# Three more chunks' low parts loaded ahead of a branch, and a prefetch hint for the branch, in an attention and two-expert-layer kernel

## The chip, the cores and the metric

The kernel runs on one core of one Trainium2 chip, in one launch. The metric is the time of an execution on the device in microseconds (us). Three runs of the kernel before gave 924.8, 921.22 and 925.86 us; their median, 924.8 us, is the time before. The engines are PE (TensorE: matmuls, with its weight loads listed as PEld), DVE (VectorE), ACT (ScalarE), POOL (GpSimd) and SP (SyncE, which issues nearly all DMAs). Each runs its own list of instructions in order and waits on semaphores for the others.

## The reference

The input goes through three layers. What is computed, cut to its core:

```python
# 1 linear attention: 4 batches, 8 heads, 576 positions, 64 wide, 128 random features
phi = lambda x: exp(x @ omega.T - (x*x).sum(-1)/2 - rowmax) / sqrt(128)
x = (phi(q) @ (phi(k).T @ v)) / (phi(q) @ phi(k).sum(0) + 1e-6)      # 2304 tokens x 512
# 2 a dense layer, hidden width 2048
h = x @ w_in
x = (h - tanh(h)) @ w_out
# 3 eight experts with room for 288 tokens each
logits = x @ w_gate
# all (token, expert) pairs by falling logit: a token goes to the first expert
# that still has room; then out[mask] = relu(x[mask] @ w1[e]) @ w2[e]
```

## The kernel before

**Precision.** Matmuls take operands as pairs: a high part, rounded to the matmul's format, and a low part, the rest. A product is three matmuls: high by high, high by low, low by high. So a name often stands twice: `gH` and `gL` are the high and low parts of a hidden chunk, `wo` and `oL` those of a chunk of `w_out`, `wi` and `iL` those of `w_in`. The low parts of the weights lie in HBM as `low_wi` and `low_wo`; a chunk's 256 KB are loaded into a ring of three buffers (`iL`, `oL`) when the chunk is due.

**The dense layer.** The 2304 tokens are six blocks of 384 (`NBLK`), a block three tiles of 128 (`TPB`); the hidden width is 16 chunks of 128 (`NF`). Per chunk `chunk_ops` makes the hidden values from 12 matmuls (L601 to L603) and a polynomial in place of `h - tanh(h)`, `hidden_ops` splits them (L298 the high part, L303 the low part, on POOL or DVE), and `m2_ops` multiplies them by the chunk of `w_out`: nine matmuls of 512 columns (L648), three into each of three accumulators `acc`.

**The last two blocks.** Blocks 4 and 5 make their hidden chunks together, before a branch; what they yield is kept. Block 5's lie in buffers of their own (`gH5`, `gL5`). Block 4's high parts overwrite the chunk of `wi` that was just used, and its low parts go to HBM (L799, `g4l<-gL`), out of a ring of four buffers `gL`, and are read back (L821, `gL<-g4l`) when the second product of block 4 needs them. This second product is `but_last_ops`: chunks 0 to 2 (`NHERE = 3`) are multiplied ahead of the branch, chunks 3 to 15 behind it, and then block 5's 16 chunks in `last_ops`: 261 matmuls of L648 behind the branch. The gate logits of both blocks don't wait for it: `last_logits` (L719, L721) takes them from the hidden parts, chunk by chunk, and after the last chunk copies, transposes (L732) and adds them into `lg` (L736, L737).

**The branch.** The polynomial holds only for small values. `range_ops` works out a flag `over` in time, and at L1455 every engine loads it into a register (TENSOR_LOAD) and at L1456 compares and branches: with `over` above 0 into a block that computes the dense layer again in a general way, otherwise past it. With these inputs the general block is jumped over. In the program's memory it stands between the code ahead of the branch and the code behind it, and has some 1,860 matmuls and other instructions of PE.

**Behind the branch.** The routing (`best_ops`, `search_ops`, `route_ops`) settles the experts one after the other, p = 0 to 7. Each search has seven steps: DVE makes thresholds and compares (`r_cmp`, L1029), PE counts (L1035, nine matmuls `rp`), DVE turns the counts into a digit (`r_cond`), PE spreads it (L1060), DVE makes the next thresholds. PE runs matmuls of L648 between these steps. After search 0 the expert's weights are loaded (`load_ops`), the tokens get their places, the rows of `ms` are gathered by POOL (L1288, `r_xg`), transposed on PE (L1304) and go through the expert's two layers (`expert_ops`, first matmul L1332).

**What sets the order.** All of it is recorded as operations with a due time (`plan.at` plus a lag) and estimated durations. `Plan.run` then issues them one by one: the operation that can start earliest, and among equals the one due first. It picks the engine where there is a choice (POOL or DVE for a low part) and the buffer of a ring; an operation without a free buffer is not ready. So a change of a ring or of a due time moves instructions far from the place that was edited. The branch ends a run of the plan: nothing moves across it.

Of the kernel before, what the change touches and what calls it, by code (L numbers as in the profile page):

```python
# [8 lines left out]
F32 = mybir.dt.float32  # L9
F32R = mybir.dt.float32r  # L10
# [175 lines left out]
def tile_kernel(ctx, tc, q, k, v, omega, w_in, w_out, w_gate, w_gate_t, w1, w2, out, dbg=None):  # L186
    nc = tc.nc
# [4 lines left out]
    P = 128  # L192
    NT, DM = v.shape
# [72 lines left out]
    def sring(where, shape, dtype, name, n):  # L266
        return plan.ring(shape, dtype, name, [(where, [f"{name}{i}" for i in range(n)], False)])
# [14 lines left out]
                    sring(wat, [P, DM], F32R, "lw", 2))  # L282
    sqr = sring(wat, [P, DM], BF16, "sq", 1)
    iLr = sring(wmid, [P, DM], F32R, "iL", 3)
    oLr = sring(wout, [P, DM], F32R, "oL", 3)
    xHr = sring(wmid, [P, NC, BLK], F32R, "xH", 2)
    xLr = sring(wmid, [P, NC, BLK], F32R, "xL", 2)
    ur = sring(wmid, [P, BLK], F32, "u", 1)
    sr = sring(wmid, [P, BLK], F32, "s", 5)
    gHr = sring(wmid, [P, BLK], F32R, "gH", 2)  # L290
    gLr = sring(wkeep, [P, BLK], F32R, "gL", 4)
    xmr = sring(wout, [P, DM], F32, "xm", 3)
    g5r = [plan.ring([P, BLK], F32R, n, []) for n in ("gH5", "gL5")]
    mTr = sring(wmid, [P, NC, P], F32, "mT", 1)
# [422 lines left out]
    def last_logits(j, acc, f, prev, gH, gL):  # L717
# [20 lines left out]
                    w=[lgb], lag=8.9)  # L738
        return o

    LAG2, LEADX, LEADI, LEADO = 10.4, 15, 5.43, 4.91

    def mlp_ops(start, step, general=False):

        x, lacc, lprev = {}, Buf(kvr), None
        for b in acc4:
            b.slot[4] = None
        for j in range(NBLK - 1):
            for i in range(j, j + 1 if j < NBLK - 2 else NBLK):
                x[i] = Buf(xHr), Buf(xLr)  # L750
                for t in range(TPB):
                    plan.at = start[j] + (3.0 if i > j else -LEADX) + 1.5 * t
                    if i == j > 0 and not general:
                        plan.at = max(x_due[i * TPB + t] + 9.0, start[j - 1] + LEADX)
                    x_ops(i, t, *x[i], general)
            if j == NBLK - 2:
                break
            acc = [Buf(accr) for _ in range(TPB)]
            prev = None
            e0, e1 = ROWS.get(j, (0, 0))  # L760
            along = not general and e0 < e1
            if along:
                plan.at = start[j]
                rows, scratch = vg_rows(e0, e1 - e0, weight_rings[0]), Buf(weight_rings[2])
            for f in range(NF):
                plan.at = start[j] + step[j] * f - LEADI
                wsp = split_ops("wi", f)
                g = Buf(gHr), Buf(gLr)
                plan.at = start[j] + step[j] * f
                chunk_ops(j, f, x[j], wsp, general, *g)  # L770
                plan.at = start[j] + step[j] * f + LAG2 - LEADO
                wsp = split_ops("wo", f)
                if along:
                    vg_ops(f, e0, e1 - e0, rows, wsp[1], weight_rings[1], scratch)
                plan.at = start[j] + step[j] * f + LAG2
                prev = m2_ops(f, g, wsp, acc, prev)
            if along and e1 == E:
                vg_split()
            for t in range(TPB):
                plan.at = start[j] + step[j] * NF + LAG2 + 0.7 * t  # L780
                xm, _ = out_ops(j, t, acc[t])
                gate_ops(j, t, xm)

        j, lacc4, lprev4 = NBLK - 2, Buf(bank), None
        for f in range(NF):
            plan.at = start[j] + step[j] * f - LEADI
            wsp = split_ops("wi", f)
            if not general:
                g5.append((Buf(g5r[0]), Buf(g5r[1])))
            plan.at = start[j] + step[j] * f  # L790
            s4 = chunk_ops(j, f, x[j], wsp, general)
            plan.at += step[j] / 2
            chunk_ops(j + 1, f, x[j + 1], wsp, general, *g5[f])
            plan.at = start[j] + step[j] * f
            gH, gL = Buf(None, wi[:, f, :BLK]), Buf(gLr)
            gH.readers = list(wbuf["wi", f].readers)
            hidden_ops(s4, gH, gL)
            lprev4 = last_logits(j, lacc4, f, lprev4, gH, gL)
            g4[f] = gH, plan.op(SP, 0.47, lambda e, f=f, gL=gL: nc.sync.dma_start(g4l[f], gL.t.bitcast(F32)), r=[gL],  # L799
                                nbytes=P * BLK * 4, lag=6.8)  # L800
            plan.at += step[j] / 2
            lprev = last_logits(j + 1, lacc, f, lprev, *g5[f])

        new = [Buf(accr) for _ in range(TPB)]
        for b in new:
            b.left += 1
        for b, old in zip(new, acc4):
            b.want = old.slot
        acc4[:] = new
        but_last_ops(0, NHERE, start[j] + step[j] * NF + 1.0, 2.0)  # L810

    g4, acc4, prev4 = {}, [], [None]
    NHERE = 3

    def but_last_ops(f0, f1, start, step):

        for f in range(f0, f1):
            plan.at = start + step * f
            gH, st = g4[f]
            gL = Buf(gLr)  # L820
            plan.op(SP, 0.47, lambda e, f=f, gL=gL: nc.sync.dma_start(gL.t.bitcast(F32), g4l[f]), w=[gL], after=[st],  # L821
                    nbytes=P * BLK * 4)
            prev4[0] = m2_ops(f, (gH, gL), split_ops("wo", f), acc4, prev4[0] if f else [flags[-1]] * TPB)

    stored, stored4, m5 = [], [], []

# [623 lines left out]
    range_ops()  # L1450
    plan.at = T_MLP + 100.0
    plan.op("-", 0.0, lambda e: r_setup(), after=flags[:1])
    plan.run()
    s_pre.close()
    nover = nc.values_load(over[0:1, 0:1], min_val=0, max_val=1)  # L1455
    with tc.If(nover > 0), ExitStack() as s_gen:  # L1456
        wgen = pool(s_gen, "wgen", "left")
        gen[:] = [sring(wgen, [P, H, D], F32, "gx", 2), sring(wgen, [P, BLK], F32, "gd", 3)]
        gsum, gmask = sring(wgen, [P, DM], F32, "gw", 1), sring(wgen, [P, DM], F32, "gm", 1)
        grings = sring(wgen, [P, DM, 2], U32, "gr", 1), gsum, sring(wgen, [P, DM], F32R, "gl", 1)  # L1460
        zeros = wgen.tile([P, DM], F32, name="zeros")
        plan.op(DVE, 0.3, lambda e: nc.vector.memset(zeros, 0.0))
        plan.at = -300.0
        for f in range(NF):
            for kind in ("wi", "wo"):
                plan.at += 4.0
                weight_ops(kind, f, grings, (gmask, zeros))
        plan.run()
        bvg[0] = Buf(None)
        for e0 in range(0, E, 2):  # L1470
            plan.at += 10.0
            rows, scratch = vg_rows(e0, 2, grings[0]), Buf(grings[2])
            for f in range(NF):
                plan.at += 2.0
                vg_ops(f, e0, 2, rows, split_ops("wo", f)[1], gsum, scratch)
            plan.run()
        vg_split()
        mlp_ops([70.0 * j for j in range(NBLK)], [4.3] * NBLK, True)
        plan.run()
# [9 lines left out]
    plan.at = -100.0  # L1489
    AT_LAST, AT_W = -42.7, 1.09  # L1490
    but_last_ops(NHERE, NF, AT_LAST - 1.5 * NF, 1.5)
    for b in acc4:
        b.left -= 1
    but_ops = list(plan.ops)
    plan.at = AT_LAST
# [97 lines left out]
```

## Time and profile before

| what | us |
|---|---|
| median of three runs | 924.8 |
| the profiled execution | 925.26 |
| its span, first to last instruction | 923.5 |
| PE busy in the span | 881.9 (95%) |
| PE's weight loads busy | 774.0 (84%) |
| DVE busy | 655.3 (71%) |
| ACT busy | 467.5 (51%) |
| POOL busy | 251.4 (27%) |

Times in the rows further down are from the span's start, so the branch is at about 546. A timeline row gives start, duration, engine, line, operation, what is written and read, and in brackets how long the engine sat idle before it and what ended that. PE's matmuls are pipelined: a row's duration includes the fill, and what one costs in a row of equals is the distance between starts. The granted clock (PEclk) is the share of full speed that TensorE was given: 1.00 is 2.4 GHz, 0.50 is 1.2 GHz.

### The profile page before, as it was taken

The numbers are of one execution on the slowest core, as the hardware profiler recorded it, in microseconds if no ns is written. First come the engines' busy times: TensorE is split into PE (matmuls) and PEld (weight loads), VectorE is DVE, ScalarE is ACT, GpSimd is POOL, SyncE is SP. The second block draws the span as 40 slices with busy tenths as digits, with TensorE's granted clock in tenths as the row PEclk, the third lists the DMA queues.
The fourth block names the chain that finished last, engine by engine and source line by source line (L and its number), as shares of the span: only waits on it lengthen the run. The fifth ranks groups of instructions, "written<-read, shape, count | busy, mean of one in ns | idle before, by whom it ended". The sixth has DMA issues, their size and how long they took to land. (4 is left out here: it accounts for less than half of the span.)

```text
span 923.5 us, 17550 instructions
## 1 busy us (share of the span) xinstructions
PE 881.9 (95%) x6168; PEld 774.0 (84%) x6168; DVE 655.3 (71%) x1931; ACT 467.5 (51%) x1015; POOL 251.4 (27%) x271
## 2 busy tenths in 40 slices
PE   8988999999999999999999949899999999999995
PEld 6887888988988888989989926676888888999995
DVE  6998999866588789777878754516787786784520
ACT  5875564645457445654577630203366454465521
POOL 1122424333431346234313230010222322221211
PEclk9997999999999999999999978999999999999998
DMA  8987877776375766434677645744798887877600
GB/s 255 345 278 237 273 242 266 264 242 206 111 239 150 217 206 218 147 104 136 233 270 269 242 152 162 270 138 156 231 272 227 271 209 214 268 180 273 211 27 26
DMA packets 104371, 194.79 MB, mean 211 GB/s; under 512 B 28369, under 2 KB 42833, under 8 KB 104274
## 3 DMA queue, kind: packets, MB, share of 16 engines
q1 hardware_dynamic: 98610, 174.71, 57.8%
q0 software_dynamic: 5664, 18.88, 8.5%
q8 instruction: 50, 0.82, 0.4%
q14 instruction: 47, 0.39, 0.1%
HBM read 150.03 MB, written 34.08 MB: 199 GB/s over the span
## 5 line engine op out<-in xcount | busy, mean ns | idle before, releaser
L601 PE MATMUL bk<-xH,wi 128*128 128x384 f32 x320 | 114.9, 359 | 1.2 <-ACT phi L438 1.0
L648 PE MATMUL acc<-wo,gL 128*128 128x512 f32 x288 | 115.5, 403 | 0.0
L602 PE MATMUL bk<-xL,wi 128*128 128x384 f32 x320 | 109.0, 341 | 0.5 <-DVE xL L303 0.5
L603 PE MATMUL bk<-xH,iL 128*128 128x384 f32 x320 | 108.9, 340 | 0.0
L707 DVE SCALAR_TENSOR_TENSOR lw<-wf,raw 128x512 f32<-128x512 f32 x128 | 103.6, 809 | 2.1 <-POOL wf L704 0.7
L648 PE MATMUL acc<-wo,gH 128*128 128x512 f32 x240 | 100.5, 419 | 0.0
L303 POOL TENSOR_TENSOR gL<-s,gH 128x384 fp32r<-128x384 f32 x52 | 63.0, 1212 | 135.9 <-ACT gH L298 128.4
L438 ACT ACTIVATE phi<-bk,nm 128x128 f32<-128x128 f32 x272 | 76.9, 379 | 38.8 <-DVE nm L441 38.5
L648 PE MATMUL acc<-oL,gH 128*128 128x512 f32 x240 | 95.5, 398 | 0.3 <-DVE oL L303 0.3
L704 POOL TENSOR_TENSOR wf<-oL,wo 128x512 f32<-128x512 f32 x48 | 64.9, 1352 | 68.0 <-DMA oL<-low_wo 61.9
L626 DVE SCALAR_TENSOR_TENSOR s<-s,bk 128x384 f32<-128x384 f32 x80 | 44.0, 551 | 45.7 <-ACT s L625 45.0
L298 ACT ACTIVATE gH<-s 128x384 fp32r<-128x384 f32 x80 | 42.2, 527 | 60.4 <-DVE s L628 43.8
L601 PEld LDWEIGHTS bk<-xH,wi 128*128 128x128 f32 x320 | 61.2, 191 | 7.3 <-ACT phi L438 2.0
L648 PEld LDWEIGHTS acc<-wo,gL 128*128 128x128 f32 x288 | 55.0, 191 | 13.2 <-POOL gL L303 0.3
L602 PEld LDWEIGHTS bk<-xL,wi 128*128 128x128 f32 x320 | 61.4, 192 | 3.3 <-DVE xL L303 0.7
L605 ACT ACTIVATE u<-bk 128x384 f32<-128x384 f32 x80 | 39.1, 489 | 46.2 <-PE bk L603 45.3
L603 PEld LDWEIGHTS bk<-xH,iL 128*128 128x128 f32 x320 | 61.2, 191 | 0.0
L628 DVE SCALAR_TENSOR_TENSOR s<-s,u 128x384 f32<-128x384 f32 x80 | 56.3, 704 | 1.1
L441 DVE TENSOR_REDUCE nm<-bk 128x4 f32<-128x512 f32 (+1 forms) x75 | 46.4, 632 | 12.9 <-PE bk L427 12.1
L648 PEld LDWEIGHTS acc<-wo,gH 128*128 128x128 f32 x240 | 45.4, 189 | 6.9
L625 ACT ACTIVATE s<-u,qbias 128x384 f32<-128x384 f32 x80 | 49.3, 616 | 3.8 <-DVE gL L303 1.5
L648 PEld LDWEIGHTS acc<-oL,gH 128*128 128x128 f32 x240 | 45.5, 190 | 6.4 <-DVE oL L303 0.6
(355 smaller groups left out, 2354.9 us busy)
## 6 DMA issues: line engine op xcount, KB each, us to landing
r_wraw<-in_moe_w_dram SPq DMA_DIRECT2D x48, 512.0 KB, 5.5
iL<-low_wi SPq DMA_DIRECT2D x80, 256.0 KB, 2.7
oL<-low_wo SPq DMA_DIRECT2D x80, 256.0 KB, 2.8
raw<-in_moe_w_in_dram SPq DMA_DIRECT2D x32, 512.0 KB, 5.6
raw<-in_moe_w_out_dram SPq DMA_DIRECT2D x32, 512.0 KB, 4.8
dw<-in_moe_w_dram SPq DMA_DIRECT2D x16, 512.0 KB, 5.0
w1l<-dw SPq DMA_DIRECT2D x16, 512.0 KB, 3.4
s_wraw<-in_moe_w_dram SPq DMA_DIRECT2D x16, 512.0 KB
```

The source lines that it names most:

```text
L303: (nc.gpsimd if e == POOL else nc.vector).tensor_tensor(out, in_, high.bitcast(F32), op=OP.subtract)
L438: nc.scalar.activation(ph.t[:, i0 + i, :], pj.t[:, i * M:(i + 1) * M], AF.Exp, bias=nmx.t[:, i0 + i:i0 + i + 1])
L441: plan.op(DVE, 0.1 + 0.125 * n, lambda e, pj=pj, i0=i0, n=n: V.tensor_reduce(nmx.t[:, i0:i0 + n], pj.t[:, :n * M].rearrange("p (i m) -> p ...
L601: nc.tensor.matmul(ph(), piece(iH, c), xH.t[:, c, :], start=(c == 0), stop=False)
L602: nc.tensor.matmul(ph(), piece(iH, c), xL.t[:, c, :], start=False, stop=False)
L603: nc.tensor.matmul(ph(), piece(iL, c), xH.t[:, c, :], start=False, stop=(c == NC - 1))
L625: plan.op(ACT, 0.52, lambda e: nc.scalar.activation(s.t, ut(), AF.Square, bias=qbias), r=[u], w=[s], lag=2.8)
L626: plan.op(DVE, 0.52, lambda e: V.scalar_tensor_tensor(s.t, s.t, QD, ph(), op0=OP.add, op1=OP.mult), r=[p, s], w=[s], lag=3.4)
L628: plan.op(DVE, 0.65, lambda e: V.scalar_tensor_tensor(s.t, s.t, QC, ut(), op0=OP.mult, op1=OP.mult), r=[u, s], w=[s], lag=4.0)
L648: nc.tensor.matmul(acc[t].t, (gL if k == 2 else gH).t[:, c], (oL if k == 1 else oH).t, start=(f == 0 and k == 0), stop=(f == NF - 1 and k ...
L704: plan.op(POOL, 1.45, lambda e: nc.gpsimd.tensor_tensor(w.t, lo.t.bitcast(F32), wo[:, f, :].bitcast(F32), op=OP.add), r=[lo, wbuf["wo", f] ...
L707: x_reads.append(plan.op(DVE, 0.9, lambda e, i=i: nc.vector.scalar_tensor_tensor(scratch.t.bitcast(F32), w.t, 1.0, half(rows[i // 2], i % ...
```

## The change

Two things. First, the low parts of chunks 3, 4 and 5 of block 4 (the `gL` read back from HBM and the `oL` of the weights) are loaded in the plan's run ahead of the branch, by `chunk_loads`, and kept across it in their buffers. For that the rings `gL` and `oL` get buffers that last (`Lasting`), and the general block is made to end with the same buffers in use. Second, a prefetch hint for the branch: the branch gets the label `range`, and `mark_branch_hint_location` marks it as likely taken, in the plan after the square of the 91st of the 96 hidden chunks (`HINT`).

```diff
-    oLr = sring(wout, [P, DM], F32R, "oL", 3)
+    oLr = sring(Lasting(wout), [P, DM], F32R, "oL", 3)
-    gLr = sring(wkeep, [P, BLK], F32R, "gL", 4)
+    gLr = sring(Lasting(wkeep), [P, BLK], F32R, "gL", 4)
+    HINT = NBLK * NF - 6
         but_last_ops(0, NHERE, start[j] + step[j] * NF + 1.0, 2.0)
-
-    g4, acc4, prev4 = {}, [], [None]
-    NHERE = 3
+        held = [b for f in sorted(ahead) for b in ahead[f]]
+        for f in range(NHERE, NHERE + NAHEAD):
+            plan.at = start[j] + step[j] * NF + 2.0 * f
+            ahead[f] = chunk_loads(f)
+        for k, b in enumerate(b for f in sorted(ahead) for b in ahead[f]):
+            b.left += 1
+            if held:
+                b.want = held[k].slot
+
+    g4, acc4, prev4, ahead = {}, [], [None], {}
+    NHERE, NAHEAD = 3, 3
+
+    def chunk_loads(f):
+
+        gL = Buf(gLr)
+        plan.op(SP, 0.47, lambda e: nc.sync.dma_start(gL.t.bitcast(F32), g4l[f]), w=[gL], after=[g4[f][1]],
+                nbytes=P * BLK * 4)
+        return gL, split_ops("wo", f)[1]
 
     def but_last_ops(f0, f1, start, step):
 
         for f in range(f0, f1):
             plan.at = start + step * f
-            gH, st = g4[f]
-            gL = Buf(gLr)
-            plan.op(SP, 0.47, lambda e, f=f, gL=gL: nc.sync.dma_start(gL.t.bitcast(F32), g4l[f]), w=[gL], after=[st],
-                    nbytes=P * BLK * 4)
-            prev4[0] = m2_ops(f, (gH, gL), split_ops("wo", f), acc4, prev4[0] if f else [flags[-1]] * TPB)
+            gL, oL = ahead[f] if f in ahead else chunk_loads(f)
+            prev4[0] = m2_ops(f, (g4[f][0], gL), (wbuf["wo", f], oL), acc4, prev4[0] if f else [flags[-1]] * TPB)
...
+    plan.op("-", 0.0, lambda e: tc.mark_branch_hint_location(
+        "range", hint="LikelyTaken", engines=list(mybir.ALL_ENGINES)), after=flags[HINT:HINT + 1])
     plan.run()
     s_pre.close()
     nover = nc.values_load(over[0:1, 0:1], min_val=0, max_val=1)
-    with tc.If(nover > 0), ExitStack() as s_gen:
+    with tc.If(nover > 0, label="range"), ExitStack() as s_gen:
...
+        for two in ahead.values():
+            for b in two:
+                b.slot[4] = None
...
     but_last_ops(NHERE, NF, AT_LAST - 1.5 * NF, 1.5)
-    for b in acc4:
+    for b in acc4 + [b for two in ahead.values() for b in two]:
         b.left -= 1
```

The lines of code behind the change are 13 to 15 higher than before (L1035 becomes L1048, L1456 becomes L1471, L821 becomes L827). In the built program the hint does not stand where the plan issues it: on each of the five engines BRANCH_PREFETCH_HINT is the second instruction of all, ahead of the first matmul, copy or DMA.

What moves, at three places. SP's queue ahead of the branch, before (`g4l` stores of block 4's last chunks, `over` the flag):

```order
L799 DMA g4l_92<-gL_6542 128x384
L799 DMA g4l_93<-gL_6566 128x384
L799 DMA g4l_94<-gL_6568 128x384
L799 DMA g4l_95<-gL_6576 128x384
L799 DMA g4l_96<-gL_6580 128x384
L1455 TENSOR_LOAD over
L1455 ISA x2
L1456 COMPARE_AND_BRANCH
```

and after (`oL<-low_wo` and `gL<-g4l` are the six loads of chunks 3 to 5):

```order
L563 DMA oL_1381<-low_wo_139 128x512
L827 DMA gL_1065<-g4l_84 128x384
L800 DMA g4l_93<-gL_1491 128x384
L563 DMA oL_1472<-low_wo_140 128x512
L800 DMA g4l_94<-gL_1026 128x384
L800 DMA g4l_95<-gL_1448 128x384
L563 DMA oL_1441<-low_wo_141 128x512
L800 DMA g4l_96<-gL_1491 128x384
L827 DMA gL_1026<-g4l_85 128x384
L827 DMA gL_1448<-g4l_86 128x384
L1470 TENSOR_LOAD over
L1470 ISA x2
```

The six loads stand among the last stores, and two of them behind the last store and ahead of the flag's load. The store of chunk 12 (`g4l_93`) comes two loads later, and chunk 15 (`g4l_96`) now leaves from the same buffer (`gL_1491`) as chunk 12.

DVE ahead of the branch, before (`lg` the logits, `gL<-s` the low part of a chunk):

```order
L303 TENSOR_TENSOR gL_6576<-s_6500,wi 128x384
L736 COPY lg<-bk_6591 128x24
L737 TENSOR_TENSOR lg<-lg,bk_6591 128x24
L736 COPY lg<-bk_6601 128x24
L737 TENSOR_TENSOR lg<-lg,bk_6601 128x24
L1455 TENSOR_LOAD over
```

and after:

```order
L303 TENSOR_TENSOR gL_1448<-s_6368,wi 128x384
L736 COPY lg<-bk_6455 128x24
L737 TENSOR_TENSOR lg<-lg,bk_6455 128x24
L303 TENSOR_TENSOR gL_1491<-s_6410,wi 128x384
L736 COPY lg<-bk_6468 128x24
L737 TENSOR_TENSOR lg<-lg,bk_6468 128x24
L1470 TENSOR_LOAD over
```

The low part of block 4's last chunk, which was POOL's last instruction ahead of the branch, is DVE's now. It goes into the buffer from which chunk 12 is stored, and so waits for that store to land.

PE behind the branch, before (`rp` the counts of the first search step):

```order
L732 MATMUL bk_11765<-ident,lt_153 128x16 x3
L1456 UNCONDITIONAL_BRANCH x2
L1035 LDWEIGHTS pairs_11780
L1035 MATMUL rp_11808<-r_cmp_11793,pairs_11780 40x62
L1035 LDWEIGHTS pairs_11780
```

and after (three accumulators by high, low and high part of chunk 3, then chunk 4):

```order
L732 MATMUL bk_11424<-ident,lt_153 128x16 x3
L1471 UNCONDITIONAL_BRANCH x2
L648 MATMUL acc_1404<-wo,wi 128x512
L648 MATMUL acc_1404<-oL_1381,wi 128x512
L648 MATMUL acc_1404<-wo,gL_1065 128x512
L648 MATMUL acc_1409<-wo,wi 128x512
L648 MATMUL acc_1409<-oL_1381,wi 128x512
L648 MATMUL acc_1409<-wo,gL_1065 128x512
L648 MATMUL acc_1397<-wo,wi 128x512
L648 MATMUL acc_1397<-oL_1381,wi 128x512
L648 MATMUL acc_1397<-wo,gL_1065 128x512
L648 MATMUL acc_1404<-wo,wi 128x512
```

Twelve matmuls of L648 (ten are shown) now stand ahead of the first count. Further on the lists differ too: up to the last digit of search 0 PE has 111 matmuls of L648 where it had 90, and from there to the first matmul of expert 0 it has 150 where it had 171; the transposes of the gathered rows (nine of L1304) stand behind the first digit of search 1, where 39 matmuls of L648 and two counts stood between; and the stores of block 4's rows (`ms<-xm`) stand ahead of the first load of expert 0's weights on SP, where they stood behind four of them.

## Rows read from the trace of the kernel before

**Rows 1.** Stretches: from:to us, length, PE busy (instructions), PEclk, DMA share, GB/s.

```profile
536.00:540.00 4.00, 4.00 (x11) 0.57 0.46 180
546.00:550.00 4.00, 0.00 (x0) 0.59 0.06 16
550.00:555.00 5.00, 0.66 (x9) 0.50 0.65 168
597.00:601.00 4.00, 3.71 (x10) 0.61 1.00 389
656.00:866.00 210.00, 209.31 (x1758) 1.00 0.79 239
```

**Rows 2.** Timeline around the branch: start, us, engine, line, operation [idle before it <- releaser].

```profile
542.75 1.09 POOL L303 TENSOR_TENSOR gL<-s,wi 128x384 fp32r<-128x384 f32 x1 [1.14 <-PE acc L648]
...
544.40 0.34 PE L721 MATMUL bk<-gL,vgs 128*8 128x384 f32 x1
...
545.30 0.35 PE L732 MATMUL bk<-ident,lt 16*128 16x16 f32 x3 [0.57 <-ACT lt L298]
...
545.91 0.18 DVE L737 TENSOR_TENSOR lg<-lg,bk 128x24 f32<-128x24 f32 x1
...
550.88 0.30 DVE L988 TENSOR_REDUCE r_m<-lg 128x18 f32<-128x144 f32 x1 [4.79 <-DVEq L1456]
...
554.23 0.66 PE L1035 MATMUL rp<-r_cmp,pairs 128*40 128x62 bf16 x9 [8.57 <-DVE pairs L992]
```

**Rows 3.** The branch's line: queue, operation, count: ns min/median/max, first and last start us.

```profile
L1456 PEldq COMPARE_BRANCH  x1: 3762/3762/3762, 545.9 to 545.9; - x1
...
L1456 DVEq COMPARE_BRANCH  x1: 72/72/72, 546.5 to 546.5; - x1
...
L1456 PEldq EVENT_SEMAPHORE  x1: 51/51/51, 549.7 to 549.7; - x1
L1456 DVEq EVENT_SEMAPHORE  x1: 21/21/21, 550.3 to 550.3; - x1
```

**Rows 4.** POOL's timeline: a low part that waits for its buffer's store.

```profile
536.21 1.09 POOL L303 TENSOR_TENSOR gL<-s,wi 128x384 fp32r<-128x384 f32 x1 [2.44 <-DMA g4l<-gL]
```

**Rows 5.** The chain that ended last, behind the branch: start, us, what, count.

```profile
555.63 4.14 PE acc L648 x9
...
564.37 0.37 PE rp L1035 x9
...
568.73 0.37 PE rp L1035 x9
...
597.46 3.74 PE acc L648 x9
...
611.07 5.69 PE acc L648 x24
```

**Rows 6.** PE's timeline from search 0's last digit to expert 0's first matmul.

```profile
583.57 0.17 PE L1060 MATMUL rp<-id,r_d 8*128 8x8 bf16 x1
...
596.22 0.51 PE L1035 MATMUL rp<-r_cmp,pairs 128*40 128x62 bf16 x9 [1.98 <-DVE pairs L992]
...
609.43 1.64 PE L1304 MATMUL bd<-ident,r_xg 128*128 128x128 f32 x9
...
634.12 0.17 PE L1060 MATMUL rp<-id,r_d 8*128 8x8 bf16 x1
...
636.99 0.19 PE L1124 MATMUL rp<-r_M,onesb 128*128 128x36 bf16 x1
...
644.02 0.41 PE L1332 MATMUL bd<-r_xgH,wi 128*128 128x288 f32 x1
```

**Rows 7.** Indices and gathers of expert 0's rows: DVE's timeline, the tile's answer, its landing.

```profile
592.66 0.29 DVE L1221 SCALAR_TENSOR_TENSOR r_ix<-r_rn,r_rp 128x1 int32<-128x1 f32 x3
...
L1288 POOL DMA_INDIRECT r_xg<-ms,r_ix x3: 877/957/1154, 600.5 to 603.3; - x3
...
DMA to landing us min/median/max: 7.0/7.0/7.0
```

## Prediction

> **What bounds the kernel now.** I read the stretches first: between 656 and 866 us, most of the expert phases, PE is busy for 209.31 of 210 us at a granted clock of 1.00 [rows 1]. So PE sets the end, and what is won ahead of it lasts as long as PE has no new wait. Then I looked for the stretches where PE does little: 546 to 550 with no matmul at all, 550 to 555 with 0.66 us, both around the branch [rows 1]. The timeline there [rows 2] shows the row to begin with: PE's counts at 554.23 had an idle time of 8.57 us before them, put down to DVE's `pairs`. But DVE itself began only at 550.88, held for 4.79 us by its own branch. The branch's line says why [rows 3]: PE's COMPARE_BRANCH lasts 3.76 us (545.9 to 549.7), DVE passes from 546.5 to 550.3, also 3.8 us, though its branch instruction takes 0.07. So PE's hole has two parts: about 3.8 us in which the branch's target is fetched, and 554.23 - 549.75 = 4.5 us in which PE has passed but its first instruction waits for DVE's four operations up to `pairs`, while the matmuls of L648 stand behind it in order.
>
> The Trainium skill, "Runtime: NRT & Kernel Launch", section Instruction fetch mechanics, says that prefetch is purely sequential and that a taken branch whose target lies outside the window forces a fetch before execution goes on. The 3.76 us agree with the second half; the first half, taken to the letter, speaks against the hint, and is rival 1 below.
>
> A third effect is in the clock. After a wait of about 2 us or more PE gets about half of full speed for a while: 0.57 from 536 to 540, 0.61 from 597 to 601, 0.59 and 0.50 around the branch [rows 1]. Nine matmuls of L648 then take 3.74 us (after a wait of 1.98 us) or 4.14 (after the branch) [rows 5, 6], and 24 at full clock 5.69, or 0.237 each, 2.13 for nine [rows 5]: a spell costs 1.6 us after a short wait, 2.0 after the long one.
>
> **The change part by part.** The sum follows PE at three points: its start behind the branch, the last digit of search 0 (call it D), and the first matmul of expert 0. Before, they are at 554.23, D = 583.57 and 644.02 [rows 2, 6].
>
> *Reaching the branch: 1.2 us later.* Block 4's last low part was made by POOL at 542.75 [rows 2]. Now DVE makes it, in the buffer from which chunk 12 is stored. The order puts two loads ahead of that store on SP, which wait for PE to have read their buffers at about 541.9, so it goes out near 542.4; a low part that waited for such a store elsewhere lost 2.44 us [rows 4]. DVE then starts near 544.9 and ends at 545.5, where POOL ended at 543.84. L721, ACT's copy, L732 and the last `lg` follow it one for one (544.40 to 546.09 [rows 2]), so the whole chain moves by 545.5 + 0.1 - 544.40 = 1.2 us. Bounds: 0 if the store is not late, 2.4 if it waits once more. SP has three loads more to issue before its flag and passes later still, but what it loads behind the branch is chunk 6 and on, 27 matmuls away.
>
> *The fetch.* The trace has no hinted branch. Bounds: 0.07 us, DVE's branch instruction by itself, and 3.76 as now [rows 3]; more than that only if the hint takes something from the code ahead (rival 3). I take 0.07 for the main case, since a fetch that has been made leaves only the instruction, and 3.76 for rival 1.
>
> *Work for the gap.* Behind the branch PE no longer waits for `pairs`: twelve matmuls of chunks 3 and 4 stand first, and their operands, issued on SP ahead of the branch, land in the 2.4 us that such a transfer takes [rows 4]. With the hint PE starts at 545.9 + 1.2 + 0.07, about 547.3; without at 551.0. The twelve take 2.8 us at full and 5 at half clock, DVE's way to `pairs` took 554.2 - 550.3 = 3.9 [rows 2, 3]; so the counts follow almost without a gap, and the cover costs nothing.
>
> *To D.* A step of the search is 568.73 - 564.37 = 4.36 us with 15 matmuls of L648 [rows 5], so its own part is 4.36 - 15 x 0.237 = 0.80. Now 111 matmuls stand before D: 111 x 0.237 + 7 x 0.80 = 31.9 us, and a spell of slow clock of 1.6 (hint) or 2.0 (none). D is at 547.3 + 31.9 + 1.6 = 580.8 with the hint, at 551.0 + 31.9 + 2.0 = 584.9 without. The clock term could vanish, as PE's pause would be shorter than any before a slow stretch here, or stay at 2.0.
>
> *From D to expert 0.* Before: 60.45 us [rows 6]. Now 150 matmuls instead of 171: -5.0. Four counts that are split around matmuls of L648: a pair of switches costs (0.80 - 0.48) / 2 = 0.16 from the step's own part less its counts (0.37) and digit (0.11), together +0.6. The wait for `pairs` of search 1 (1.98 us [rows 6]) and its slow spell stay, as DVE's order there is unchanged. The first digit of search 1 has only four counts and no matmul to cover DVE: +0.2. The transposes of the gathered rows now come about 17 us behind D instead of 609.43 - 583.57 = 25.9 [rows 6]. The gathers wait for the indices, 592.66 + 0.29, D + 9.4, and start 2.8 us apart from first to last [rows 7]; the third lands at D + 9.4 + 2.8 + 7.0 = D + 19.2 if it takes the 7.0 us of the row [rows 7], a wait of 2.2 us, or none if it takes 4. I take 0.7. At the end search 1 finishes one digit later against the matmuls: between its last digit and L1124 lie 2.87 us [rows 6], which eight matmuls of L648 covered and now nine small ones of about 1.2; half of the 1.7 left was waited for elsewhere before, so +0.9. Together -5.0 + 0.6 + 0.2 + 0.7 + 0.9 = -2.6, so 57.85 us. Bounds: -4.4 (only the splits cost) and +0.6 (the full wait of 2.2 and another slow spell of 1.6).
>
> *The sum.* With the hint expert 0 starts at 580.8 + 57.85 = 638.7, 5.3 us earlier. Behind it the work is the same and PE has no idle time to lose it in [rows 1]; weights of expert 1 are asked for later against PE, which I price at nothing because the loads have several us of lead, and at 2 if that is used up. The profiled execution took 925.26 us; less 5.3 it is 920.0. The median of the runs is 0.46 below that execution, so I forecast 919.5.
>
> **The rivals.** *1, the hint does nothing:* prefetch follows the sequence, or takes the general block, which follows the branch anyway. For it: the hint stands at the very start of each engine's code, hundreds of microseconds ahead of its branch. Against it: it names this branch, and nothing in the rows says that it would be forgotten. PE starts at 551.0 and expert 0 at 584.9 + 57.85 = 642.75, 1.3 us earlier: 924.0, or 923.5 as a median. The skill's sentence on sequential prefetch gives this same time.
>
> *2, the transposes take the gain:* the gathered rows land later than PE comes, at full price 2.2 us and a slow spell of 1.6 rather than 0.7: 3.1 us more. With the hint 922.6. It speaks for it that the gathers run while the weights of expert 0 fill the queues (DMA share 1.00 from 597 to 601 [rows 1]); against it that the stores they wait for now leave ahead of those loads.
>
> *3, the hint harms, slower than before:* the place that the target takes is missing to the code in sequence, and PE's fetches ahead of the branch are no longer early. A fetch that is waited for costs 3.76 us each time [rows 3]. One would leave the case of rival 1 at 927; from two on the kernel is slower than 930. Nothing in the rows speaks for it but the hint's early place.
>
> **How the numbers follow.** Main case 0.48, rival 1 0.33, rival 2 0.12, rival 3 0.07. The main case's own range is 916 to 923, from its bounds: 3.6 better if the slow spell is gone and only the splits cost, 3.2 worse if the late terms reach theirs. Rival 1 has 920 to 927. A range of 915.5 to 926.5 leaves out about a tenth of each of these and rival 3. Within 0.5% of 924.8, which is about what a measurement of this kernel can tell from no change, means 920.2 to 929.4: the main case lies below it in six of ten, rival 1 in two of ten and rival 2 in one of ten, together 0.37; slower, 0.08, is rival 3 and the end of rival 1; the rest, 0.55, is the same. I put faster at 0.38 and same at 0.54.
>
> **What would show it.** The hint: PE's COMPARE_BRANCH below 0.5 us, and DVE's EVENT_SEMAPHORE as close behind its branch. The late last chunk: DVE's last `lg` near 547.3. The filled gap: L648 as PE's first row behind the branch, and the counts without a wait of several us for `pairs`. D near 580.8, or 584.9 without the hint. The transposes: a wait at L1317 for the gather, below or above 2 us. Expert 0's first matmul near 638.7. I am wrong if the branch still takes 3.8 us, if PE has new idle time behind 650 of more than 2 us, or if stretches ahead of 530 are longer than before.

## The result, and the profile after

The changed kernel takes 935.16 us (median of 6 runs, 934.14 to 939.11), the kernel before 922.61 beside it; the ratio is 1.014, with an interval of 1.0113 to 1.0166. It is slower by 12.5 us, where 5.3 less was forecast. Its profiled execution, the longest of the six, took 939.11 us, span 937.0.

The program is cut at the prediction's own points: the last transpose of logits ahead of the branch (L732), the last digit of search 0 (D), expert 0's first matmul, the end. The row "forecast" has the prediction's values; the rows under it are profiled executions of the experiments below.

| kernel | to last L732 | L732 to D | D to expert 0 | expert 0 to end | span |
|---|---|---|---|---|---|
| before | 545.30 | 38.27 | 60.45 | 279.5 | 923.5 |
| forecast | 546.5 | 34.3 | 57.85 | 279.5 | 918.2 |
| after | 549.97 | 39.26 | 58.24 | 289.5 | 937.0 |
| hint_only | 544.56 | 33.62 | 60.40 | 278.6 | 917.2 |
| loads_only | 544.86 | 40.00 | 58.26 | 289.5 | 932.6 |
| after_e0first | 547.55 | 39.89 | 58.16 | 282.7 | 928.3 |
| after_dve7 | 549.22 | 39.68 | 58.29 | 282.7 | 929.9 |
| nahead1 | 543.27 | 31.99 | 60.13 | 283.2 | 918.6 |
| nahead1_e0first | 547.19 | 32.50 | 59.45 | 280.5 | 919.6 |
| h2a1 | 542.37 | 31.88 | 60.22 | 278.4 | 912.9 |
| h1a2 | 543.71 | 36.21 | 59.70 | 280.4 | 920.0 |
| h2a1_hold | 543.13 | 33.90 | 60.39 | 278.6 | 916.0 |
| hint_pe | 547.68 | 36.29 | 60.45 | 279.4 | 923.8 |

Against the forecast, two columns fail: 5.0 us at the branch and 10.0 behind expert 0's start. The first column is mostly chance: the first matmul of L601 starts at 56.8 us in the profiled executions of after and after_dve7, and at 50.9 to 52.0 in all others, with the same code ahead of it, and in after 3.0 us of that are left at the last L601. Each row is one execution, so times are compared by their medians, and traces by the other columns.

**The branch.** The branch's line in the trace of after (queue, operation, count: ns, first and last start):

```profile
L1471 SPq EVENT_SEMAPHORE  x8: 17/17/17, 553.5 to 555.4; - x8
...
L1471 PEldq COMPARE_BRANCH  x1: 392/392/392, 550.7 to 550.7; - x1
...
L1471 SPq COMPARE_BRANCH  x1: 70/70/70, 552.0 to 552.0; - x1
L1471 DVEq EVENT_SEMAPHORE  x1: 21/21/21, 552.0 to 552.0; - x1
```

The hint works: PE's branch lasts 0.39 us instead of 3.76, DVE passes 0.6 us after its branch instead of 3.8 [rows 3]. But SP comes last now. It reaches its own branch at 552.0 and then waits on eight semaphores, which its transfers use in turn, the last at 555.4. In the trace of before the same row of SP was over before PE and DVE had passed (549.7 and 550.3), so it cost nothing:

```profile
L1456 SPq EVENT_SEMAPHORE  x8: 17/17/17, 548.3 to 548.8; - x8
```

The timeline of after around it, which answers to [rows 2]:

```profile
548.45 0.56 DVE L303 TENSOR_TENSOR gL<-s,wi 128x384 fp32r<-128x384 f32 x1 [0.68 <-DMA g4l<-gL]
...
549.97 0.49 PE L732 MATMUL bk<-ident,lt 16*128 16x16 f32 x3 [0.57 <-ACT lt L298]
550.25 5.70 SPq L827 DMA_DIRECT2D gL<-g4l  x3
...
551.33 0.77 PE L648 MATMUL acc<-wo,wi 128*128 128x512 f32 x1 [0.86 <-PEq L1471]
555.50 0.76 PE L648 MATMUL acc<-oL,wi 128*128 128x512 f32 x1 [3.41 <-SPq L1471]
...
555.64 0.30 DVE L1001 TENSOR_REDUCE r_m<-lg 128x18 f32<-128x144 f32 x1 [4.74 <-SPq L1471]
```

PE issues one matmul behind the branch and then waits 3.41 us for SP; DVE waits 4.74 for it. SP's row at 550.25 joins three issues of `gL<-g4l`, the first two, at 550.25 and 550.74, ahead of the flag's load. The line of the trace on these two loads:

```profile
DMA to landing us min/median/max: 3.2/3.7/4.2
```

So they land at 553.5 and 554.9. SP passes its first semaphore at 553.5, the second at 555.0 and the other six within 0.5 us: it is these two loads that it waits for.

**Behind expert 0's start.** PE's timeline of after, which answers to [rows 6]:

```profile
589.23 0.17 PE L1073 MATMUL rp<-id,r_d 8*128 8x8 bf16 x1
...
606.76 1.50 PE L1317 MATMUL bd<-ident,r_xg 32*128 32x32 f32 x7 [0.21 <-DMA r_xg<-ms,r_ix]
...
643.97 0.17 PE L1073 MATMUL rp<-id,r_d 8*128 8x8 bf16 x1
...
647.47 0.38 PE L1345 MATMUL bd<-r_xgH,wi 128*128 128x288 f32 x1
...
651.34 0.40 PE L1347 MATMUL bd<-r_xgH,s_ewL 128*128 128x288 f32 x1 [1.38 <-DMA s_ewL<-w1l]
...
679.54 0.61 PE L1366 MATMUL bd<-s_hH,s_ewL 128*128 128x288 f32 x1 [4.01 <-DMA s_ewL<-r_wraw]
```

Search 1's last digit comes 3.5 us ahead of expert 0's first matmul (643.97, 647.47); before it was 9.9 (634.12, 644.02 [rows 6]). Behind it stand two waits for weights of expert 0, 1.38 and 4.01 us, where before had none. The clock follows the second wait (stretches of after: from:to us, length, PE busy, PEclk, DMA share, GB/s):

```profile
550.00:555.00 5.00, 1.23 (x4) 0.50 0.57 176
555.00:560.00 5.00, 4.50 (x11) 0.51 0.21 50
...
680.00:690.00 10.00, 10.00 (x48) 0.52 0.33 106
```

Ten us at a granted clock of 0.52 do the work of 5.2, so the second wait and its clock make 4.0 + 4.8 = 8.8 of the 10.0 us of the column. The first wait is made good: of the 1,536 matmuls of 288 columns from expert 0's first one on, the 150th starts 27.5 us behind the first in after and 27.3 in before, the 200th 47.9 and 38.6.

Why are the weights late? SP's timeline, first of before, then of after:

```profile
636.72 2.51 SPq L660 DMA_DIRECT2D ms<-xm  x3
639.43 0.34 SPq L1260 DMA_DIRECT2D s_ewL<-w1l  x1
```

```profile
638.45 4.16 SPq L660 DMA_DIRECT2D ms<-xm  x3
646.62 0.34 SPq L1273 DMA_DIRECT2D s_ewL<-w1l  x1
```

In after 4.0 us lie between the last store and the next load. There SP's list has the register load of expert 1's number (`r_ei`), which DVE makes only after search 1, and four loads of expert 0's weights stand behind it. SP's register load in after:

```profile
L1255 SPq TENSOR_LOAD <-r_ei x1: 270/270/270, 645.8 to 645.8; - x1
```

In before the four loads stood behind it as well, but search 1 was over by then. POOL's timeline shows the second queue, again before, then after:

```profile
661.65 1.06 POOL L1288 DMA_INDIRECT r_xg<-ms,r_ig  x1 [13.80 <-DVE r_pre L1042]
662.69 0.97 POOL L1267 DMA_DIRECT2D s_ewL<-r_wraw  x1
```

```profile
666.33 1.18 POOL L1301 DMA_INDIRECT r_xg<-ms,r_ig  x1 [6.95 <-DVE r_cmp L1042]
667.81 1.00 POOL L1301 DMA_INDIRECT r_xg<-ms,r_ig  x1 [0.30 <-DVE r_base L1062]
668.79 1.04 POOL L1280 DMA_DIRECT2D s_ewL<-r_wraw  x1
```

POOL's transfer of expert 0's last low part stands behind gathers of expert 1's rows, whose indices also come from search 1. ACT, which makes what it adds to, is done at 664.9 in after, 3.9 us before it goes out. In before it goes out 18.7 us after expert 0's start, in after 21.3, and in the chain that ended last it is a piece of its own (start, us, what; the first row is PE's behind the branch):

```profile
555.50 4.79 PE acc L648 x11
...
668.79 10.71 DMA s_ewL<-r_wraw
```

### The profile page after: what moved, and what is told of

The parts are those of the page before. It is cut to its first block, busy times and chain, and to the rows that moved or that the text cites. A ratio compares the mean times of both kernels' runs of the same rounds, so it can differ in the third digit from the quotient of the medians.

```text
span 937.0 us, 17555 instructions
## 1 busy us (share of the span) xinstructions
PE 893.0 (95%) x6168; PEld 783.1 (84%) x6168; DVE 653.6 (70%) x1930; ACT 468.7 (50%) x1017; POOL 251.1 (27%) x270
## 5 line engine op out<-in xcount | busy, mean ns | idle before, releaser
L648 PE MATMUL acc<-wo,gL 128*128 128x512 f32 x288 | 116.3, 405 | 0.0
L601 PE MATMUL bk<-xH,wi 128*128 128x384 f32 x320 | 114.1, 357 | 0.8 <-DVE xt L500 0.5
L648 PE MATMUL acc<-wo,gH 128*128 128x512 f32 x240 | 100.4, 420 | 0.0
L648 PE MATMUL acc<-oL,gH 128*128 128x512 f32 x240 | 95.9, 400 | 0.3 <-DVE oL L303 0.3
L648 PEld LDWEIGHTS acc<-wo,gL 128*128 128x128 f32 x288 | 55.5, 193 | 13.1 <-POOL gL L303 0.2
L601 PEld LDWEIGHTS bk<-xH,wi 128*128 128x128 f32 x320 | 60.8, 190 | 6.2 <-PE bk L480 0.7
L628 DVE SCALAR_TENSOR_TENSOR s<-s,u 128x384 f32<-128x384 f32 x80 | 52.1, 651 | 1.1
L648 PEld LDWEIGHTS acc<-wo,gH 128*128 128x128 f32 x240 | 45.9, 191 | 7.5 <-issue 0.3
L648 PEld LDWEIGHTS acc<-oL,gH 128*128 128x128 f32 x240 | 46.0, 192 | 6.5 <-DVE oL L303 0.6
```

The costliest lines, as they stand in the source:

```text
L601: nc.tensor.matmul(ph(), piece(iH, c), xH.t[:, c, :], start=(c == 0), stop=False)
L628: plan.op(DVE, 0.65, lambda e: V.scalar_tensor_tensor(s.t, s.t, QC, ut(), op0=OP.mult, op1=OP.mult), r=[u, s], w=[s], lag=4.0)
L648: nc.tensor.matmul(acc[t].t, (gL if k == 2 else gH).t[:, c], (oL if k == 1 else oH).t, start=(f == 0 and k == 0), stop=(f == NF - 1 and k ...
```

## The experiments

The theory was: the hint is a gain; the loads in flight make SP hold every engine; and search 1, late against the matmuls, makes expert 0's weights late. All ratios are to the kernel before.

**hint_only: the kernel before with the hint alone.**

```diff
+    HINT = NBLK * NF - 6
...
+    plan.op("-", 0.0, lambda e: tc.mark_branch_hint_location(
+        "range", hint="LikelyTaken", engines=list(mybir.ALL_ENGINES)), after=flags[HINT:HINT + 1])
...
-    with tc.If(nover > 0), ExitStack() as s_gen:
+    with tc.If(nover > 0, label="range"), ExitStack() as s_gen:
```

> The kernel before with the label and the hint alone; no load is moved, so the order on every engine stays that of before. Theory (the hint is worth what the branch no longer costs, down to the moment at which SP has waited out its transfers): PE passes its branch at about 546.3 instead of 549.7 and DVE at 547.1 instead of 550.3; SP, whose own branch was passed at 548.3, now waits only for its last store, issued at 544.2 and landing near 546.6. DVE's first reduction starts at about 547.1 instead of 550.88, the last digit of search 0 is 3.7 us earlier, nothing behind it gets a new wait: about 3.6 us faster than before, 919.0 against 922.6. Rival (the hint itself harms, by slowing the code ahead of the branch): 922.6 or more, and the stretch ahead of 530 longer. Second rival (SP's hold takes the gain): release at 548.8 as now, 1 to 1.5 us faster.

919.88 us, ratio 0.9959 (0.9939 to 0.9979). The branch's line and the timeline of hint_only:

```profile
L1459 SPq EVENT_SEMAPHORE  x8: 17/17/17, 545.2 to 545.8; - x8
...
L1459 PEldq COMPARE_BRANCH  x1: 392/392/392, 545.2 to 545.2; - x1
...
L1459 DVEq EVENT_SEMAPHORE  x1: 21/21/21, 546.4 to 546.4; - x1
```

```profile
547.00 0.30 DVE L989 TENSOR_REDUCE r_m<-lg 128x18 f32<-128x144 f32 x1 [1.65 <-DVEq L1459]
...
549.31 0.65 PE L1036 MATMUL rp<-r_cmp,pairs 128*40 128x62 bf16 x9 [4.39 <-DVE pairs L993]
```

SP is done at 545.8, DVE last at 546.4: nobody waits long for anybody. PE's hole from its last L732 to the first counts is 4.75 us instead of 8.93. The first theory holds; the hint does no harm.

**loads_only: the changed kernel without hint and label.**

```diff
-    plan.op("-", 0.0, lambda e: tc.mark_branch_hint_location(
-        "range", hint="LikelyTaken", engines=list(mybir.ALL_ENGINES)), after=flags[HINT:HINT + 1])
...
-    with tc.If(nover > 0, label="range"), ExitStack() as s_gen:
+    with tc.If(nover > 0), ExitStack() as s_gen:
```

> The changed kernel without the hint and the label: the loads of three chunks ahead of the branch alone. Theory (at the branch SP's wait for the loads in flight is the last to end, so the hint bought nothing in the changed kernel): PE passes at 550.7 + 3.8 = 554.5, DVE at 551.4 + 3.8 = 555.2, about when SP lets go (555.5): 935, within 1 us of the changed kernel. Rival (the hint is a cost of the changed kernel): 931 or less. Second rival (the hint still saves its 3.7 us there): 938.5.

936.17 us, ratio 1.0144 (1.0115 to 1.0174), the same as after. Its branch's line and timeline:

```profile
L1469 SPq EVENT_SEMAPHORE  x8: 17/17/17, 550.6 to 551.1; - x8
...
L1469 PEldq COMPARE_BRANCH  x1: 4065/4065/4065, 545.5 to 545.5; - x1
...
L1469 SPq COMPARE_BRANCH  x1: 50/50/50, 547.0 to 547.0; - x1
```

```profile
551.19 0.77 PE L648 MATMUL acc<-oL,wi 128*128 128x512 f32 x1 [0.71 <-SPq L1469]
```

The time is the expected one, and PE's branch, 4.07 us here, ends before SP lets go. But the reason is another than the theory's. The line of the trace on the last two loads, issued at 545.3 and 545.8:

```profile
DMA to landing us min/median/max: 3.1/3.5/3.8
```

They have landed by 549.6, a us before SP's first semaphore at 550.6. Without a hint SP's own passage takes 3.6 us (547.0 to 550.6; 2.6 in before), and that is what ends last here. With the hint it takes 0.5 (h2a1), and then the loads end last, as in after. So in after the hint has bought close to nothing: PE's second matmul starts 5.5 us behind the last L732, and 6.3 here.

**after_e0first: SP's register load for expert 1 behind all loads of expert 0.**

```diff
-    ew = {}
+    ew, loads0, LOADS0 = {}, [], 8
...
-        o = plan.op(SP, 1.2, lambda e: reg.append(nc.sync.value_load(ei.t[0:1, 0:1], min_val=0, max_val=E - 1)), r=[ei])
+        o = plan.op(SP, 1.2, lambda e: reg.append(nc.sync.value_load(ei.t[0:1, 0:1], min_val=0, max_val=E - 1)), r=[ei],
+                    after=loads0 if p == 1 else [])
...
-            plan.op(SP, 0.47, load, w=[raw], after=[o], nbytes=P * FX * 4)
+            ld = plan.op(SP, 0.47, load, w=[raw], after=[o], nbytes=P * FX * 4)
+            if p == 0 and i < LOADS0:
+                loads0.append(ld)
...
-                plan.op(SP, 0.47, load_low, w=[L], after=[o], nbytes=P * FX * 4)
+                ld = plan.op(SP, 0.47, load_low, w=[L], after=[o], nbytes=P * FX * 4)
+                if p == 0:
+                    loads0.append(ld)
```

> The changed kernel, with SP's register load of expert 1's number put behind all loads of expert 0's weights; in the plan this also puts POOL's last weight transfer of expert 0 ahead of the gathers of expert 1's rows. Theory (the 10 us behind expert 0's start come from expert 0's last weights standing behind work that waits for the end of search 1): the loads go out at about 642.7 instead of 646.6, the waits of 1.4 and 4.0 us and the slow clock behind the second (about 4.8 us) go: about 925, 10 us faster than the changed kernel. Rival (the weights are late because the transfers are slower or asked for more at once, not because of their place in the queue): the waits stay, 933 to 936.

927.91 us, ratio 1.0056 (1.0035 to 1.0077): 7.3 us less than after. SP's and POOL's timelines (the gathers now follow the transfer, from 664.24), and the largest of PE's waits behind expert 0's start (us in total, times, longest):

```profile
640.91 0.34 SPq L1276 DMA_DIRECT2D s_ewL<-w1l  x1
```

```profile
659.54 0.85 POOL L1285 DMA_DIRECT2D s_ewL<-r_wraw  x1 [10.00 <-ACT s_hH L1354]
```

```profile
PE rp L1137 <- DVE r_M L1126: 1.1, 1, 1.1
```

The load goes out 0.2 us behind the stores, POOL's transfer 13.9 us after expert 0's start (645.60), and no wait for weights is left. The lateness was one of place in the queues. Of the 10.0 us in the last column 6.8 are gone; the expected 925 was too low by 3. What is left comes late: the 800th of the 1,536 matmuls starts 152.3 us behind expert 0's first (151.5 in before, 161.4 in after), and only then, up to the 1,000th, another 2.2 us are lost (190.5 for 187.5 in before), with no wait of PE and a granted clock of 1.00. Why is not shown.

**after_dve7: expert 0's last low part by DVE instead of POOL's transfer.**

```diff
-            elif i in (BYDMA if p < PDMA else ()):
+            elif i in (BYDMA[:2] if p == 0 else BYDMA if p < PDMA else ()):
```

> The changed kernel, with the low part of expert 0's last weight chunk made by DVE from the raw chunk instead of by ACT and an adding transfer that POOL issues. Tells the two queues apart. If the place in POOL's queue, behind the gathers of expert 1's rows, makes the 4.0 us wait: that wait and the slow clock behind it go, 1.4 us at the earlier one stays, about 926 to 927. If it is SP's place, the raw chunk being late: a wait of 2 us or more stays near 676, 932 to 935.

929.04 us, ratio 1.0059 (1.0039 to 1.0078). PE's largest wait behind expert 0's start:

```profile
PE bd L1347 <- DMA s_ewL<-w1l: 1.8, 1, 1.8
```

The 4.0 us wait and its slow clock are gone, and SP's wait (1.4 in after) stays with 1.8. So the long wait was one for POOL's transfer, and after_e0first, which moves that transfer and keeps it, shows that it was its place behind the gathers; the short one was SP's place behind the register load. What is left here comes early: the 40th matmul is 2.8 us behind before (9.7 for 6.9), with the wait of 1.8 and a granted clock of 0.83 in the first ten us.

**nahead1: one chunk ahead instead of three.** 

```diff
-    NHERE, NAHEAD = 3, 3
+    NHERE, NAHEAD = 3, 1
```

> The changed kernel with one chunk loaded ahead (NAHEAD = 1), hint kept. Its two loads stand ahead of the last four stores on SP, so none is in flight when the flag comes; but block 4 and 5's matmuls still stand early: when search 1 gives its last digit only 2 matmuls of L648 are left (11 before, 1 in the changed kernel). Theory (two separate losses, loads in flight that hold every engine at the branch, and search 1 late against the matmuls so that expert 0's last weights come late): PE's wait for SP behind the branch is below 1 us instead of 3.4, the wait for expert 0's weights near 675 is still there with 2 us or more: 926 to 931. Rival (the loads in flight are the one cause of both, the order behind the branch costs nothing): no wait for weights, 919 to 921.

924.74 us, ratio 1.0017 (0.9996 to 1.0037). Half of the expectation holds: the loads leave at 537.5 and 538.4, SP's semaphores are not the last, and L732 to D takes 31.99 us. The other half does not: with search 1's last digit 7.1 us ahead of expert 0 there is no wait for weights, only 0.7 and 0.5 us for DVE. Yet its last column has 283.2, partly for a granted clock of 0.90 in the first 25 us. Its branch's line:

```profile
L1471 SPq EVENT_SEMAPHORE  x8: 17/17/17, 544.1 to 544.7; - x8
...
L1471 DVEq EVENT_SEMAPHORE  x1: 21/21/21, 545.2 to 545.2; - x1
```

**nahead1_e0first: the same with the register load behind.** It has the edits of nahead1 and of after_e0first together.

> The same with one chunk loaded ahead, and SP's register load of expert 1's number behind all loads of expert 0's weights. Theory: neither the hold nor the late weights are left; nine matmuls fill part of the gap in which PE waits for DVE: 918 to 921, at or a little below the hint alone (919.9). If the order behind the branch has a further cost that the place of the register load does not touch: 922 to 926.

922.28 us, ratio 0.9986 (0.9963 to 1.001): at the edge between the two expectations, and not told apart from before or from nahead1.

**h2a1: chunk 2 multiplied behind the branch, no load added.** 

```diff
-    NHERE, NAHEAD = 3, 3
+    NHERE, NAHEAD = 2, 1
```

> Hint, and chunk 2 multiplied behind the branch instead of ahead (NHERE = 2, NAHEAD = 1): the nine matmuls that fill the gap are ones whose operands were loaded ahead of the branch anyway, no load is added, and search 1's last digit again has 11 matmuls of L648 behind it as before. Theory: no hold by SP, no late weights; the nine matmuls of 2.1 us, moved into the 4.4 us in which PE waits for DVE in the kernel with the hint alone, are won as far as they bounded PE ahead of the branch: 917 to 919. If they only filled idle time ahead of the branch, or if the low part that waits for a store (one buffer fewer) costs as much: 919.5 to 921, as the hint alone. If a held buffer delays the chunks ahead of the branch by more than that: above 921.

918.17 us, ratio 0.9952 (0.9931 to 0.9973). PE's timeline:

```profile
543.59 0.77 PE L648 MATMUL acc<-wo,wi 128*128 128x512 f32 x1 [0.86 <-PEq L1471]
...
547.22 0.44 PE L1048 MATMUL rp<-r_cmp,pairs 128*40 128x62 bf16 x9
```

The gap at the branch is 0.86 us, the nine matmuls run to the counts without a wait. Its median is the lowest of all, below before and after by more than its interval; from hint_only (0.9959, within that interval) it is not told apart.

**h1a2: chunks 1 and 2 behind the branch.** 

```diff
-    NHERE, NAHEAD = 3, 3
+    NHERE, NAHEAD = 1, 2
```

> Hint, and chunks 1 and 2 multiplied behind the branch (NHERE = 1, NAHEAD = 2): 18 matmuls, 4.3 us, fill the gap whole, no load is added, but two buffers of the ring of four are held, so block 4's last low parts share two and wait for stores (2.4 us each where such a wait is shown). Theory: won 4 us in the gap at most, lost one or two store waits in the chain to the last logits: 917 to 922. The order behind the branch is again that of before, so no wait for weights of more than 1 us; if there is one, the search's lead is not what makes them late.

925.81 us, ratio 1.0016 (0.999 to 1.0042), slower than expected. Search 1's last digit again comes 9.9 us ahead of expert 0, and there is no wait for weights, as expected. L732 to D takes 36.21 us, 4.3 more than in h2a1, of which 12 matmuls of L648 more (111 for 99) are 2.8. But 18 matmuls fewer ahead of the branch bring the last L732 only 0.9 us forward against hint_only (543.71 for 544.56), where nine fewer in h2a1 bring 2.2. Where the rest goes was not followed up.

**h2a1_hold: two transfers more in flight.** In h2a1, behind everything else that SP issues ahead of the flag:

```diff
+    for b, src in zip(ahead[NHERE], (g4l[NHERE], lows["wo", NHERE])):
+        nc.sync.dma_start(b.t.bitcast(F32), src)
     s_pre.close()
```

> The kernel with the hint and chunk 2 multiplied behind the branch (h2a1), with two transfers added as the last on SP ahead of the flag: the gL and oL of that chunk are loaded a second time into the same buffers, with the same data. Nothing else moves. Theory (at the branch SP waits for every transfer in flight, and all engines wait for SP): SP's last semaphore, at 543.8 in h2a1, comes 2.4 to 3.5 us later relative to the last L732, PE and DVE have a row that waits for SP, and the slow clock lasts longer: 2 to 4 us slower than h2a1, 920 to 922. Rival (only the instruction count on SP matters, transfers in flight are not waited for): 0.8 us of issue and nothing in the time, 918 to 918.5.

920.39 us, ratio 0.9972 (0.9956 to 0.9989). The branch's line, and the first rows of PE and DVE behind it:

```profile
L1473 SPq EVENT_SEMAPHORE  x8: 17/17/17, 544.9 to 546.2; - x8
...
L1473 DVEq EVENT_SEMAPHORE  x1: 21/21/21, 545.0 to 545.0; - x1
```

```profile
546.15 0.76 PE L648 MATMUL acc<-oL,wi 128*128 128x512 f32 x1 [1.10 <-SPq L1473]
```

```profile
546.37 0.30 DVE L1001 TENSOR_REDUCE r_m<-lg 128x18 f32<-128x144 f32 x1 [2.45 <-SPq L1473]
```

The hold is there again, made by two transfers whose data nobody needed anew. DVE's row decides: it reads nothing that they write, and it waits 2.45 us for SP, where in h2a1 it waits 1.7 for its own passage. PE's matmul reads the `oL` that is written again, so its wait could be one for the data too. L732 to D takes 2.0 us more than in h2a1. The medians differ by 2.2, the ratios by 0.002, and their intervals overlap: the time alone does not show it.

**hint_pe: the hint on PE's list alone.** In hint_only:

```diff
-        "range", hint="LikelyTaken", engines=list(mybir.ALL_ENGINES)), after=flags[HINT:HINT + 1])
+        "range", hint="LikelyTaken", engines=[mybir.EngineType.PE]), after=flags[HINT:HINT + 1])
```

> The kernel before with the hint on PE's list alone. Theory (behind the branch DVE's four operations up to pairs set the first count, so DVE's own passage, 3.8 us without a hint, is what counts, and PE's cut from 3.76 to 0.39 by itself is worth nothing): PE's branch lasts 0.4 us and DVE's passage still 3.8; 922 to 924, no change from before. Rival (PE's fetch was the bound, as its line in the profile suggests): 919.5 to 920.5, as with the hint on all engines.

922.45 us, ratio 0.9978 (0.9955 to 1.0002): no change that can be told. The branch's line and PE's timeline:

```profile
L1459 PEldq COMPARE_BRANCH  x1: 397/397/397, 548.3 to 548.3; - x1
...
L1459 DVEq COMPARE_BRANCH  x1: 72/72/72, 548.9 to 548.9; - x1
...
L1459 DVEq EVENT_SEMAPHORE  x1: 21/21/21, 551.8 to 551.8; - x1
```

```profile
554.72 0.65 PE L1036 MATMUL rp<-r_cmp,pairs 128*40 128x62 bf16 x9 [6.68 <-DVE pairs L993]
```

PE passes early and waits 6.68 us for DVE, whose own passage still takes 2.9, though not the 3.8 that were expected. The longest branch in the profile was not the one that set the end. Not all of the gain is lost in this trace: PE's hole from the last L732 to the counts is 7.04 us instead of 8.93, 0.9 of it by DVE's shorter passage; the medians don't tell.

## Why the prediction was wrong

*Reaching the branch, 1.2 us later:* right. DVE makes the last low part and waits for the store (the row at 548.45). From the last L601 (529.2 and 532.2) to the last L732 it is 16.1 us in before and 17.7 in after: 1.6.

*The fetch:* right for the main case. 0.39 us on PE instead of the 0.07 taken. Rival 1 (the hint does nothing) and rival 3 (it harms) fall; hint_only shows it alone. The prediction cited the Trainium skill, "Runtime: NRT & Kernel Launch", section Instruction fetch mechanics, for a taken branch that waits for its target: 4.07 us in loads_only agree. That prefetch is purely sequential, as the page says, the runs do not bear out for a hinted branch; the measurement decides.

*Work for the gap, where "the cover costs nothing":* this step failed. The sentence "SP has three loads more to issue before its flag and passes later still, but what it loads behind the branch is chunk 6 and on", in the part on reaching the branch, asked what SP does behind the branch, and not who waits for SP there. PE, DVE and POOL do, and SP waits for its transfers. It also took the 2.44 us of [rows 4], which are a wait, for the time of a transfer; the last two loads took 3.2 and 4.2. The price is 3.41 us of PE's time; in 550 to 560 the clock stays at 0.50, so that eleven matmuls take 4.79 us in the chain, where 11 x 0.237 = 2.6 would do: 2.2 for the spell that was put at 1.6. L732 to D was forecast at 34.3 and took 39.26. In nahead1, where SP's semaphores are not the last and 99 matmuls stand ahead of D, the prediction's own formula gives 0.8 + 99 x 0.237 + 7 x 0.80 + 1.6 = 31.5, and 31.99 was measured: the other terms are sound. That its spell "could vanish" with a short pause did not come true: PE's pause at the branch is 0.8 us there, and from 543 to 548 the granted clock is 0.66.

*From D to expert 0:* right, 58.24 for 57.85. The transposes waited 0.21 us, rival 2 falls. The sum is in part luck: the wait for `pairs` stayed (1.85 us), but from 607 to 611 there is a second slow stretch (granted clock 0.58) that the main case did not have, so the terms it did have must have come out lower together.

*The sum, where late weights were priced "at nothing because the loads have several us of lead, and at 2 if that is used up":* this step failed, and it is the larger one, 10.0 us. The prediction saw its cause ("search 1 finishes one digit later against the matmuls") and followed it only on PE, for 0.9 us. It spoke of expert 1's weights; the ones that came late were expert 0's. It did not look at what else waits for search 1 and what stands behind that: on SP a register load with expert 0's loads behind it, on POOL the gathers with expert 0's last transfer behind them. after_e0first and after_dve7 each take 6.8 of the 10.0 away. The remaining 3 arise at different places in the two, as said above, and only those of after_dve7 have a cause that is seen. That "behind it the work is the same" is not quite so either: 11 matmuls more, nine of them one step's counts, stand behind expert 0's start.

## What to carry to other kernels

Behind a branch an engine may go on only when another has passed too: when a change speeds up one, look in the branch's line for the next, and count the transfers that an engine waits out as part of its passage. Here loads issued just ahead of the branch cost more than they gave; work whose operands were there anyway filled the gap without a wait (h2a1). When a step becomes late against the engine that bounds, list all queues that wait for it, and for each what stands behind the wait, even if that work has nothing to do with the step.

## What the runs showed that was not expected

- A hint that stands as the second instruction of an engine's list, some 545 us ahead of its branch, still cuts PE's branch from 3.76 to 0.39 us, and does so in each of the hinted runs (388 to 397 ns).
- Each engine's passage is its own: without a hint DVE's takes 2.9 us (hint_pe), 3.8 (before) and 4.5 (loads_only, 546.1 to 550.6) though its branch instruction lasts 0.07, and SP's 2.6 (before) and 3.6 (loads_only). With the hint on PE's list PE's branch is down to 0.40 and DVE's passage still 2.9.
- With two transfers in flight at the branch, whose data nobody needs, DVE waits 2.45 us for SP; without them it waits 1.7 for its own passage.
- A wait of 4.01 us was followed by ten us at a granted clock of 0.52: the clock cost more than the wait.
